# Top-32 attention and a tanh-shrink FFN: engine order written out by hand, search on pairs of keys, tanh subtraction on GpSimd

## The chip, the cores and the metric

The kernel runs on one core of a Trainium2 chip, in float32 throughout. The metric is the device time of one execution in microseconds. Engines are named as in the profile: PE (TensorE matmuls), PEld (its weight loads), DVE (VectorE), ACT (ScalarE), POOL (GpSimd), SP (SyncE, here a queue for DMA issues).

## What is computed

```python
# q, k, v: (8, 8, 576, 64) float32: batches, heads, positions, head dimension
scores = (1/8) * q @ k^T
kth = 32nd largest of each row of 576 scores
scores = where(scores >= kth, scores, -1e9) - max of the row
attn = exp(scores) / (sum + 1e-9)
x = (attn @ v), transposed to (4608, 512)
# w_in (512, 2048), w_out (2048, 512): 64-bit floats
h = x @ w_in
out = (h - tanh(h)) @ w_out
```

## The kernel before, in words

The attention part is a row of 144 steps. A step is one block of 128 queries of two heads (a pair, `hp`) of one batch: 16 such steps in a batch, four query blocks for each of four pairs. 576 is 4 x 128 + 64, so the last 64 queries of two pairs are put together in a step of their own (`g.rem`), two of them in a batch.

`turn_kq` transposes keys and queries of a pair on PE. `scores` (L181) computes a step's scores for both heads into `scps`, a PSUM tile of four banks with one buffer (`sc_ps`), and ACT copies it to `sc` in SBUF. `top` (L200) finds the 32 largest of each row's 576 on DVE: four rounds of MAX8, which gives the eight largest, with a MATCH_REPLACE8 between rounds that overwrites those eight. For two heads that is 8 MAX8 and 6 MATCH_REPLACE8 on 576 elements. The 32nd is the threshold (`tb`, POOL); ACT and POOL push all scores under it far down (`z`), and ACT takes the exponential with its sum.

`weigh` (L240) transposes `z` on PE in nine blocks, through `zt`, PSUM tiles of one bank with two buffers (`zt_ps`, which `turn_kq` and `values` share); ACT copies them out (`et`, `e4`). After every second query block `values` (L276) multiplies with v (`av`), transposes the reciprocal sums (`rb`), and DVE writes the product into `xT`.

Two query blocks of all pairs make a unit of 256 columns for the FFN (384 where the remaining queries of two batches are added). `ffn_h` (L324) does four matmuls into an `hps` bank (two buffers, `h_ps`), ACT takes the tanh, and DVE subtracts it straight from PSUM:

```python
        nc.scalar.activation(th[:, 0:N], ps[:, 0:N], AF.Tanh)
        u.g[f] = gpool.tile([P, 3 * P], FP32, tag="g", name="g")
        nc.vector.tensor_tensor(u.g[f][:, 0:N], ps[:, 0:N], th[:, 0:N], ALU.subtract)
```

`ffn_o` (L343) multiplies with `w_out` in `ops` tiles of the same two PSUM buffers. The weights come as 64-bit floats, and `load_weights` (L101) turns each of 32 pieces of 128 x 512 into float32 with four instructions on DVE, two on ACT and two on POOL; it runs beside the first steps, with its DMAs on ACT's queue.

A loop over n writes these functions down in the order scores(n+1), top(n), weigh(n-1), values(n-1), loads, and then FFN work up to a `credit` that grows by a share in each step. That is the order in which the framework is told of the instructions. It then orders each engine's queue itself, by its own planning, and sets the semaphores; in the trace, transposes of one step stand between FFN matmuls and scores of another.

Of the kernel before, what the change touches and what calls it, by code (L numbers as in the profile page):

```python
# [16 lines left out]
TOP = 32  # L17
# [13 lines left out]
class Unit:  # L31
# [3 lines left out]
    def __init__(self, name, blocks):  # L35
        self.name, self.blocks = name, blocks
        self.N = 128 * len(blocks)
        self.xT = None
        self.g = {}
# [3 lines left out]
def kernel(  # L43
# [16 lines left out]
    S2 = S // 2  # L60
    CD = DM // P
# [5 lines left out]
    assert D == 64 and R == 64 and DM == H * D and B % 2 == 0  # L67
# [19 lines left out]
    gpool = pool("g", 16)  # L87
# [5 lines left out]
    make_identity(nc, ident[:])  # L93
    w_in = [consts.tile([P, CD, DFF // WJ], FP32, name=f"w_in{j}") for j in range(WJ)]
# [6 lines left out]
    def load_weights(j, i):  # L101
# [6 lines left out]
        raw64 = rawpool.tile([P, NW, 2], U32, tag="raw64", name="raw64")  # L108
        nc.scalar.dma_start(raw64[:].rearrange("p n w -> p (n w)"), src.bitcast(U32))
        lo, hi = raw64[:, :, 0], raw64[:, :, 1]  # L110

# [16 lines left out]
        nc.gpsimd.tensor_tensor(dst, dst, f[:], ALU.mult)  # L128

# [28 lines left out]
    def turn_kq(b, hp):  # L158
        for name, dst in (("k", kT), ("q", qT)):
# [12 lines left out]
            for rows, o in [(half(0), 0), (half(1), R)] if name == "k" else [(slice(0, P), 0)]:  # L172
                nc.scalar.copy(d[rows, o : o + JP], ps[rows, :])
                o = 0 if o else JP
                nc.scalar.copy(d[rows, o : o + R], p4[rows, 0:R])

# [4 lines left out]
    def scores(n, g):  # L181
# [16 lines left out]
        st[n] = dict(sc=sc)  # L198

    def top(n):  # L200

        sc = st[n]["sc"]
        scf = sc[:].rearrange("p t s k -> p t (s k)")
        m = mpool.tile([P, 2, TOP], FP32, tag="m", name="m")
        cur = [scf[:, t, :] for t in range(2)]
# [12 lines left out]
        tb = mpool.tile([P, 2], FP32, tag="tb", name="tb")  # L218
        nc.gpsimd.tensor_scalar(tb[:], m[:, :, TOP - 1], BIG, None, ALU.mult)  # L219

        z = zpool.tile([P, 2 * S], FP32, tag="z", name="z")
        zv = z[:].rearrange("p (t k) -> p t k", t=2)
        den = mpool.tile([P, 2], FP32, tag="den", name="den")
        for t in range(2):
            nc.scalar.activation(zv[:, t, :], scf[:, t, :], AF.Relu, bias=tb[:, t : t + 1], scale=-BIG)  # L225
        nc.gpsimd.tensor_tensor(zv, scf, zv, ALU.subtract)  # L226
        for t in range(2):
            nc.scalar.activation(  # L228
                zv[:, t, :],
                zv[:, t, :],  # L230
                AF.Exp,
                bias=nb[:, t : t + 1],
# [3 lines left out]
        st[n].update(z=z, den=den)  # L236
# [3 lines left out]
    def weigh(n, g):  # L240


        z, den = st[n]["z"], st[n]["den"]
        if g.rem:
            et = etrpool.tile([P, 2, J, P], FP32, tag="etr", name="etr")
            e4 = etrpool.tile([P, P], FP32, tag="e4r", name="e4r")
            o = 0
        else:
            o = (g.qt % 2) * P
            if o == 0:  # L250
                ets[g.hp] = (
                    etpool.tile([P, 2, J, 2 * P], FP32, tag="et", name="et"),
                    etpool.tile([P, 2 * P], FP32, tag="e4", name="e4"),
                    xpool.tile([P, 2, 2], FP32, tag="rd", name="rd"),
                )
            et, e4, rd = ets[g.hp]
            rd = rd[:, g.qt % 2, :]
        for t in range(2):
# [6 lines left out]
            nc.scalar.copy(et[:, t, :, o : o + P], zt[:].rearrange("p (c j) -> p c j", c=J))  # L265
        zt = zt_ps.tile([P, 512], FP32, tag="zt", name="zt")
        nc.tensor.transpose(zt[:, 0:P], z[:, JP : JP + P], ident[:])
        nc.scalar.copy(e4[:, o : o + P], zt[:, 0:P])
        if g.rem:
            rd = xpool.tile([P, 1, 2], FP32, tag="rdr", name="rdr")  # L270
            nc.gpsimd.tensor_scalar(rd[:, 0, :], den[:], EPS, None, ALU.add)
            return et, e4, rd
        nc.gpsimd.tensor_scalar(rd, den[:], EPS, None, ALU.add)
        return ets.pop(g.hp) if o else None

    def values(g, et, e4, rd):  # L276

        ri = xpool.tile(list(rd.shape), FP32, tag="ri", name="ri")
        nc.vector.reciprocal(ri[:], rd[:])
        rx = xpool.tile([P, 2, 2, D], FP32, tag="rx", name="rx")  # L280
        nq = 1 if g.rem else 2
# [183 lines left out]
```

## Time and profile before

| | |
|---|---|
| time, median of three runs | 2197.74 us (2193.26 to 2206.97) |
| profiled execution, its own time | 2196.81 us |
| its span in the trace | 2195.0 us |
| mean granted clock of TensorE in the span | 0.907 |
| busy share of the span | PE 82%, DVE 74%, ACT 45%, POOL 29% |

The span is what the trace covers; the rest of the execution's time, 1.8 us, lies around it. The granted clock is 1 where the throttle lets TensorE run at 2.4 GHz and 0.5 where it lets it run at 1.2 GHz, so that 0.907 is a mean over stretches of either. A matmul's record is longer than its turn on the engine, since matmuls overlap: busy time counts a moment once, and the mean of one is longer than busy time by count.

### The profile page before, as it was taken

To read this page: it belongs to the slowest core of one execution; us is meant where nothing else is said; L and a number is where in the kernel's file an instruction comes from. 1 tells how busy PE (TensorE), PEld (TensorE's weight loads), DVE (VectorE), ACT (ScalarE), POOL (GpSimd) and SP (SyncE) were. 2 spreads that over 40 slices of the span, in tenths; PEclk is the share of its full clock that TensorE was granted. 3 is DMA by queue.
4 is the path that set the end of the run, shared out by engine and by line. 5 is a ranking of instruction groups with operands and counts; after the bars stand their busy time and mean duration, and the time that the engine had idled before them with its cause. 6 is when DMAs were issued, how large, how long until landed. Compare 5 with 4: busy or idle time off the path is not lost. (4 is left out here: it accounts for less than half of the span.)

```text
span 2195.0 us, 24121 instructions
## 1 busy us (share of the span) xinstructions
PE 1799.9 (82%) x8160; PEld 1035.6 (47%) x8160; DVE 1624.4 (74%) x3440; ACT 997.5 (45%) x2069; POOL 628.4 (29%) x726
## 2 busy tenths in 40 slices
PE   3354777988888888989888988989888988888879
PEld 2222534545454464545444464646444464646444
DVE  6777677887778786878778786878778776878730
ACT  4333444454454444544554454544445444544420
POOL 5555542222223222222222222222223222222210
PEclk7555897999889999999889999999979999999989
DMA  5211111000110001000110000100100000000000
GB/s 148 61 58 58 39 51 31 14 10 5 38 33 1 15 22 37 17 10 1 43 33 1 15 23 27 28 10 1 41 24 12 10 19 24 27 11 1 10 0 15
DMA packets 102140, 56.10 MB, mean 26 GB/s; under 512 B 85121, under 2 KB 93313, under 8 KB 102017
## 3 DMA queue, kind: packets, MB, share of 16 engines
q1 hardware_dynamic: 97408, 37.78, 6.6%
q10 hardware_dynamic: 4608, 16.78, 2.4%
q8 instruction: 65, 1.06, 0.2%
q14 instruction: 59, 0.48, 0.1%
HBM read 45.09 MB, written 9.44 MB: 25 GB/s over the span
## 5 line engine op out<-in xcount | busy, mean ns | idle before, releaser
L210 DVE MAX8 m<-w 128x8 f32<-128x576 f32 x864 | 616.0, 747 | 0.0
L347 PE MATMUL ops<-w_out,g 128*128 128x512 f32 x1152 | 537.4, 609 | 19.2 <-DVE g L339 9.6
L226 POOL TENSOR_TENSOR z<-sc,z 128x1152 f32<-128x1152 f32 x144 | 381.1, 2647 | 205.8 <-issue 153.8
L329 PE MATMUL hps<-xT,w_in 128*128 128x256 f32 x1536 | 392.7, 401 | 54.9 <-DVE g L339 40.5
L214 DVE MATCH_REPLACE8 w<-m,w 128x576 f32<-128x576 f32 x576 | 427.5, 742 | 0.0
L225 ACT ACTIVATE z<-sc,tb 128x576 f32<-128x576 f32 x288 | 208.7, 768 | 328.9 <-POOL tb L219 328.7
L228 ACT ACTIVATE z<-z,nb 128x576 f32<-128x576 f32 x288 | 220.9, 768 | 286.9 <-POOL z L226 286.9
L329 PEld LDWEIGHTS hps<-xT,w_in 128*128 128x128 f32 x1536 | 291.7, 201 | 115.2 <-DVE g L339 57.6
L347 PEld LDWEIGHTS ops<-w_out,g 128*128 128x128 f32 x1152 | 214.9, 197 | 233.0 <-issue 206.3
L210 DVE MAX8 m<-sc 128x8 f32<-128x576 f32 x288 | 207.1, 747 | 151.2 <-ACT sc L197 151.1
L262 PE MATMUL zt<-ident,z 128*128 128x128 f32 x1152 | 178.3, 299 | 147.5 <-ACT z L228 143.0
L219 POOL TENSOR_SCALAR tb<-m 128x2 f32<-128x2 f32 x144 | 47.4, 329 | 846.6 <-DVE m L210 761.0
L189 PE MATMUL scps<-kT,qT 64*128 64x288 f32 (+1 forms) x1280 | 247.4, 458 | 3.7 <-ACT sc L197 3.7
L262 PEld LDWEIGHTS zt<-ident,z 128*128 128x128 f32 x1152 | 137.3, 151 | 214.1 <-ACT z L228 165.6
L214 DVE MATCH_REPLACE8 w<-m,sc 128x576 f32<-128x576 f32 x288 | 211.7, 742 | 0.0
L197 ACT COPY sc<-scps 128x1152 f32<-128x1152 f32 x144 | 159.8, 1110 | 86.0 <-PE scps L189 81.5
L339 DVE TENSOR_TENSOR g<-hps,th 128x256 f32<-128x256 f32 (+1 forms) x256 | 113.8, 451 | 108.4 <-ACT th L337 106.7
L329 PE MATMUL hps<-xTb,w_in 128*128 128x384 f32 x512 | 186.5, 507 | 7.9 <-DVE g L339 7.2
L337 ACT ACTIVATE th<-hps 128x256 f32<-128x256 f32 (+1 forms) x256 | 100.5, 407 | 200.4 <-PE hps L329 196.7
L189 PEld LDWEIGHTS scps<-kT,qT 64*128 64x128 f32 (+1 forms) x1280 | 117.2, 186 | 114.8 <-issue 87.9
L291 PE MATMUL av<-et,vb 128*64 128x256 f32 x1024 | 143.9, 430 | 9.4 <-ACT et L265 9.3
L265 ACT COPY et<-zt 128x512 f32<-128x512 f32 x256 | 139.8, 586 | 4.9 <-PE zt L262 4.5
(60 smaller groups left out, 1196.6 us busy)
## 6 DMA issues: line engine op xcount, KB each, us to landing
raw<-in_moe_w_in_dram ACTq DMA_DIRECT2D x16, 512.0 KB, 4.4
kin<-in_k_dram SPq DMA_DIRECT2D x64, 128.0 KB, 2.6
qin<-in_q_dram SPq DMA_DIRECT2D x64, 128.0 KB, 2.6
vb<-in_v_dram SPq DMA_DIRECT2D x64, 128.0 KB, 2.2
raw<-in_moe_w_out_dram ACTq DMA_DIRECT2D x16, 512.0 KB, 3.2
out_dram<-ot SPq DMA_DIRECT2D x32, 256.0 KB, 2.3
kin<-in_k_dram SPq DMA_DIRECT2D x64, 16.0 KB, 2.3
qin<-in_q_dram SPq DMA_DIRECT2D x64, 16.0 KB, 2.4
```

The costliest lines, as they stand in the source:

```text
L189: nc.tensor.matmul(ps[rows, t, s, 0:S2], qT[g.b, g.hp + i][half(t), qs], kT[g.b, g.hp + i][half(t), ks], start=True, stop=True,)
L197: nc.scalar.copy(sc[:], ps[:, :, :, 0:S2])
L210: nc.vector.max(m[:, t, m8], cur[t])
L214: nc.vector.match_replace(w[:], m[:, t, m8], cur[t], NEG)
L225: nc.scalar.activation(zv[:, t, :], scf[:, t, :], AF.Relu, bias=tb[:, t : t + 1], scale=-BIG)
L226: nc.gpsimd.tensor_tensor(zv, scf, zv, ALU.subtract)
L228: nc.scalar.activation(zv[:, t, :], zv[:, t, :], AF.Exp, bias=nb[:, t : t + 1], scale=scale, accum_out=den[:, t : t + 1],)
L262: nc.tensor.transpose(zt[:, c * P : (c + 1) * P], z[:, m0 + c * P : m0 + (c + 1) * P], ident[:])
L265: nc.scalar.copy(et[:, t, :, o : o + P], zt[:].rearrange("p (c j) -> p c j", c=J))
L291: nc.tensor.matmul(av[half(t), cols], vb[g.b, hp][:, t, c, :] if c < J else vr[g.b, hp][rows, :], et[:, t, c, cols] if c < J else e4[rows, ...
L329: nc.tensor.matmul(ps[:, 0:N], w_in[j][:, c, fo : fo + P], u.xT[:, c, 0:N], start=(c == 0), stop=(c == CD - 1),)
L347: nc.tensor.matmul(acc[u, i][:], u.g[f][:, i * P : (i + 1) * P], w_out[part][:, f % FJ, :], start=(f == 0), stop=(f == CF - 1),)
```

## The change

**Order.** The loop body stands in `manual_schedule`, which keeps each engine's queue in the order written. In step n the order is: transposes of step n-2 (two of three groups), mask of n-1, search of n, half of the step's FFN items, scores of n+1, the third group of transposes of n-2, exponentials of n-1, a quarter of the items, values of n-2, loads and turns, the last quarter. The reciprocal of step n-2 (`invert`) stands in DVE's queue inside the search of n, after its first round. An FFN item is one `ffn_h` (four matmuls) or two f of an `ffn_o`; 4.4 are dealt in a step while there are any.

**Search.** The 576 scores of a row are taken as 288 pairs (column x with column x+288). DVE takes minimum and maximum of each pair, one operand from PSUM (`ps`) and one from SBUF, so `scps` is now held until DVE has read it. The four rounds run on the 288 larger ones, and the eight largest of the smaller ones are put in for the last round: 2 TENSOR_TENSOR, 10 MAX8 and 6 MATCH_REPLACE8. Should a row have more of the smaller ones among its 32 than the eight, that is seen at the end: `b8s` against `tbs`, summed by a matmul, loaded into registers as a flag; if it is set, the whole program runs a second time with the old search (`run(True)`).

**Subtraction on GpSimd.** ACT takes tanh of two f at once (512 columns), copies `hps` to SBUF as well, and POOL subtracts. POOL also writes `xT`, from a copy that ACT makes of `av` and the reciprocals together. The remaining queries get units of their own (four batches, 256 columns), so all 18 units have 256 columns.

**Weights.** `convert` is cut in three: the DMA (now on SP's queue), a first part up to POOL's limiting of the exponent, a second part. Three pieces end in a step, from step -1 to step 10; of three pieces in a row two have both parts in the same step.

```diff
-    rawpool = pool("raw", 2)
     ldpool = pool("ld", 1)
     kqpool = pool("kq", 4)
-    scpool = pool("sc", 2)
-    wpool = pool("w", 3)
-    mpool = pool("m", 4)
+    scpool = pool("sc", 3)
+    abpool = pool("ab", 2)
+    mpool = pool("m", 3)
     zpool = pool("z", 2)
-    etpool = pool("et", 2)
-    etrpool = pool("etr", 1)
+    etpool = pool("et", 1)
     xpool = pool("x", 2)
-    xbpool = pool("xb", 1)
+    xrpool = pool("xr", 1)
     hpool = pool("h", 2)
-    gpool = pool("g", 16)
+    thpool = pool("th", 3)
+    gpool = pool("g", 6)
...
+    def convert(j, i):
...
-        nc.scalar.dma_start(raw64[:].rearrange("p n w -> p (n w)"), src.bitcast(U32))
+        raw64 = gpool.tile([P, NW, 2], U32, tag="g", name="raw64")
+        nc.sync.dma_start(raw64[:].rearrange("p n w -> p (n w)"), src.bitcast(U32))
+        yield
...
-        f = rawpool.tile([P, NW], FP32, tag="f", name="f")
-        fu = f[:].bitcast(U32)
-        nc.vector.tensor_scalar(fu, hi, 20, 0x7FF, ALU.logical_shift_right, ALU.bitwise_and)
-        nc.scalar.activation(f[:], fu, AF.Copy, bias=-896.0 * 2.0**23, scale=2.0**23)
...
+    def search(n, exact):
+        x = st[n]
+        sc, ps = x["sc"], x.pop("ps")
+        m = x["m"] = mpool.tile([P, 2, TOP], FP32, tag="m", name="m")
+        ab = abpool.tile([P, 2, S + 8], FP32, tag="ab", name="ab")
+        if exact:
+            cur = [sc[:, t].rearrange("p s k -> p (s k)") for t in range(2)]
+            nxt = [ab[:, t, 0:S] for t in range(2)]
+            last = nxt
+        else:
+            x["ab"] = ab
+            cur = nxt = [ab[:, t, 0:S2] for t in range(2)]
+            last = [ab[:, t, 0 : S2 + 8] for t in range(2)]
+            hi, lo = ab[:, :, 0:S2], ab[:, :, S2 + 8 :]
+            nc.vector.tensor_tensor(lo, ps[:, :, 0, 0:S2], sc[:, :, 1, :], ALU.min)
+            nc.vector.tensor_tensor(hi, ps[:, :, 0, 0:S2], sc[:, :, 1, :], ALU.max)
+            for t in range(2):
+                nc.vector.max(ab[:, t, S2 : S2 + 8], lo[:, t, :])
         rounds = TOP // 8
         for i in range(rounds):
             m8 = slice(8 * i, 8 * i + 8)
             for t in range(2):
-                nc.vector.max(m[:, t, m8], cur[t])
+                nc.vector.max(m[:, t, m8], last[t] if i == rounds - 1 else cur[t])
             if i < rounds - 1:
                 for t in range(2):
-                    w = wpool.tile([P, S], FP32, tag="w", name="w")
-                    nc.vector.match_replace(w[:], m[:, t, m8], cur[t], NEG)
-                    cur[t] = w[:]
+                    nc.vector.match_replace(nxt[t], m[:, t, m8], cur[t], NEG)
+                cur = nxt
+            if i == 0:
+                yield
...
+                    tbs[:, t, n : n + 1],
+                    m[:, t, TOP - 1 : TOP],
+                    m[:, t, TOP - 9 : TOP - 8],
+                    BIG,
+                    ALU.min,
+                    ALU.mult,
...
+            nc.gpsimd.tensor_tensor(zv[:, t, :], scf[:, t, :], zv[:, t, :], ALU.subtract)
+        if not exact:
+            nc.gpsimd.tensor_scalar(
+                b8s[:, :, n], x.pop("ab")[:, :, S2 + 7], BIG, None, ALU.mult
+            )
+        x.update(z=z, zv=zv, nb=nb)
...
+    def invert(n):
+        g, rd = steps[n], rds.get(n)
+        if rd is not None and (g.rem or g.qt % 2):
+            nc.vector.reciprocal(rd[:], rd[:])
...
-        nc.scalar.copy(rs[:, 0:N], rb[:, 0:N])
+                av[:, 1, i * P : (i + 1) * P], rx[:, i].rearrange("p t d -> p (t d)"), ident[:]
+            )
+        xs = xpool.tile([P, 2, N], FP32, tag="xs", name="xs")
+        nc.scalar.copy(xs[:, :, 0:w], av[:, :, 0:w])
         if g.rem:
-            u = units[g.b | 1, 1]
+            u = rests[g.b // 4]
             for i in range(2):
-                o = 2 * P + (g.b % 2) * R
-                nc.vector.tensor_tensor(
-                    xt(u)[:, g.hp + i, o : o + R], av[:, half(i)], rs[:, half(i)], ALU.mult
+                o = g.b % 4 * R
+                nc.gpsimd.tensor_tensor(
+                    xt(u)[:, g.hp + i, o : o + R], xs[:, 0, half(i)], xs[:, 1, half(i)], ALU.mult
                 )
         else:
             u = units[g.b, g.qt // 2]
-            nc.vector.tensor_tensor(xt(u)[:, g.hp, 0:N], av[:, 0:N], rs[:, 0:N], ALU.mult)
+            nc.gpsimd.tensor_tensor(xt(u)[:, g.hp, :], xs[:, 0], xs[:, 1], ALU.mult)
...
-        th = hpool.tile([P, 3 * P], FP32, tag="th", name="th")
-        nc.scalar.activation(th[:, 0:N], ps[:, 0:N], AF.Tanh)
-        u.g[f] = gpool.tile([P, 3 * P], FP32, tag="g", name="g")
-        nc.vector.tensor_tensor(u.g[f][:, 0:N], ps[:, 0:N], th[:, 0:N], ALU.subtract)
-    acc = {}
+        if f % 2:
+            th = thpool.tile([P, 2, N], FP32, tag="th", name="th")
+            if f % FJ == 1:
+                u.g.append(gpool.tile([P, FJ, N], FP32, tag="g", name="g"))
+            g = u.g[-1][:, f % FJ - 1 : f % FJ + 1, :]
+            nc.scalar.activation(th[:], ps[:], AF.Tanh)
+            nc.scalar.copy(g, ps[:])
+            nc.gpsimd.tensor_tensor(g, g, th[:], ALU.subtract)
...
+        share = 1.1 * items * 2 * CF / NS
...
+        at(-6, lambda: load_kq(*pairs[0]))
+        for i, (b, hp) in enumerate(pairs):
             n = first[b] + 2 * hp
-            at(n - 6, lambda b=b, hp=hp: load_kq(b, hp))
-            at(n - 4, lambda b=b, hp=hp: turn_kq(b, hp))
+            turn = turn_kq(b, hp)
+            at(n - 4, lambda turn=turn: next(turn))
+            at(n - 3, lambda turn=turn: next(turn))
+            if i + 1 < len(pairs):
+                at(n - 3, lambda i=i: load_kq(*pairs[i + 1]))
             at(n - 2, lambda b=b, hp=hp: load_v(b, hp))
...
+        pieces = [] if exact else [convert(j, i) for j in range(2 * WJ) for i in range(FJ)]
+        for i, piece in enumerate(pieces):
+            for s in range(3):
+                at((i + s) // 3 - 1, lambda piece=piece: next(piece))
+        credit = 0.0
+        def deal(part):
+            nonlocal credit
+            credit += part * share
+            while work and credit > 0:
+                work.pop(0)()
+                credit -= 1
+            credit = credit if work else min(credit, 0.0)
+        for n in range(-6, NS + 2):
+            here = lambda i: 0 <= n + i < NS
+            if here(-2):
+                w = weigh(n - 2)
+                next(w)
+            if here(-1):
+                mask(n - 1, exact)
+            if here(0):
+                s = search(n, exact)
+                next(s)
+                if here(-2):
+                    invert(n - 2)
+                next(s, None)
+            elif here(-2):
+                invert(n - 2)
+            deal(0.5)
+            if here(1):
+                scores(n + 1)
+            if here(-2):
+                next(w)
+            if here(-1):
+                expo(n - 1)
+            deal(0.25)
+            if here(-2):
+                values(n - 2)
+            for fn in todo.pop(n, []):
+                fn()
+            deal(0.25)
+        while work:
+            work.pop(0)()
+        return NS
+    with tc.manual_schedule():
...
+        NS = run(False)
+    bad = xpool.tile([P, 2, NS], FP32, tag="bad", name="bad")
+    nc.vector.tensor_tensor(bad[:], b8s[:], tbs[:], ALU.is_gt)
+    any_bad = xpool.tile([P, 1], FP32, tag="anybad", name="anybad")
+    nc.vector.reduce_max(any_bad[:], bad[:].rearrange("p t n -> p (t n)"), axis=mybir.AxisListType.X)
+    cnt = zt_ps.tile([P, 512], FP32, tag="zt", name="cnt")
+    nc.tensor.matmul(cnt[0:1, 0:1], any_bad[:], ones[:], start=True, stop=True)
+    flag = xpool.tile([1, 1], I32, tag="flag", name="flag")
+    nc.vector.tensor_copy(flag[:], cnt[0:1, 0:1])
+    again = nc.values_load(flag[0:1, 0:1], min_val=0, max_val=P)
+    with tc.If(again > 0):
+        with tc.manual_schedule():
+            run(True)
```

## Rows read from the trace of the kernel before

**Rows 1.** Page of before: busy us (share of the span) xinstructions.
```profile
PE 1799.9 (82%) x8160; PEld 1035.6 (47%) x8160; DVE 1624.4 (74%) x3440; ACT 997.5 (45%) x2069; POOL 628.4 (29%) x726
```

**Rows 2.** Windows, search instructions of L210 alone: start:end, us, busy (count), clock.
```profile
0.00:300.00 300.00, 75.78 (x106) 0.70 0.23 70
600.00:2000.00 1400.00, 571.38 (x804) 0.95 0.07 19
```

**Rows 3.** Windows of all engines: start:end, us, busy (count) by engine, clock.
```profile
600.00:2000.00 1400.00, 1222.67 (x5701) 707.65 (x5697) 1088.16 (x2320) 672.08 (x1404) 350.76 (x457) 0.95 0.07 19
602.00:634.00 32.00, 27.26 (x116) 16.30 (x115) 23.56 (x53) 16.42 (x34) 7.45 (x10) 0.73 0.15 38
2124.80:2190.00 65.20, 65.20 (x173) 32.40 (x171) 5.57 (x10) 6.07 (x12) 0.00 (x0) 1.00 0.02 8
```

**Rows 4.** Waits of PE from 600 to 2000 us: total us, times, longest.
```profile
PE zt L267 <- ACT et L265: 50.0, 29, 5.2
PE zt L262 <- ACT z L228: 28.7, 14, 5.0
PE hps L329 <- DVE g L339: 26.7, 26, 2.1
```

**Rows 5.** Groups by form, 600-2000 us: count, busy us, mean ns, idle.
```profile
L210 DVE MAX8 m<-w 128x8 f32<-128x576 f32 x604 | 431.9, 747 | 0.0
L347 PE MATMUL ops<-w_out,g 128*128 128x512 f32 x800 | 371.4, 605 | 7.3 <-DVE g L339 7.3
L214 DVE MATCH_REPLACE8 w<-m,w 128x576 f32<-128x576 f32 x403 | 299.2, 742 | 0.0
L329 PE MATMUL hps<-xT,w_in 128*128 128x256 f32 x1096 | 273.3, 395 | 23.3 <-DVE g L339 19.5 <-DVE xT L314 3.6
L226 POOL TENSOR_TENSOR z<-sc,z 128x1152 f32<-128x1152 f32 x101 | 265.6, 2630 | 138.7 <-issue 113.4 <-POOL nb L217 25.2
...
L329 PE MATMUL hps<-xTb,w_in 128*128 128x384 f32 x376 | 137.7, 504 | 7.2 <-DVE g L339 7.2
...
L265 ACT COPY et<-zt 128x512 f32<-128x512 f32 x178 | 97.1, 585 | 1.3 <-PE zt L262 1.0
...
L339 DVE TENSOR_TENSOR g<-hps,th 128x256 f32<-128x256 f32 x136 | 56.2, 419 | 37.9 <-ACT th L337 36.9
...
L339 DVE TENSOR_TENSOR g<-hps,th 128x384 f32<-128x384 f32 x48 | 26.0, 548 | 25.0 <-ACT th L337 24.8
```

**Rows 6.** Timeline 1000 to 1032 us: one run of FFN matmuls at full clock.
```profile
1009.66 5.45 PE L329 MATMUL hps<-xT,w_in 128*128 128x256 f32 x24 [1.52 <-DVE g L339]
```

**Rows 7.** Groups of the weight conversion, whole span.
```profile
L122 POOL TENSOR_SCALAR f<-f 128x512 int32<-128x512 f32 x32 | 62.1, 1950 | 15.1 <-ACT f L121 13.6
...
L125 DVE SCALAR_TENSOR_TENSOR f<-raw,f 128x512 uint32<-128x512 uint32 x32 | 30.9, 967 | 78.6 <-POOL f L122 78.4
...
L128 POOL TENSOR_TENSOR w_in<-w_in,f 128x512 f32<-128x512 f32 x16 | 20.7, 1292 | 5.3 <-DVE f L125 5.1
...
L121 ACT ACTIVATE f<-f 128x512 f32<-128x512 uint32 x32 | 19.1, 617 | 6.7 <-DVE f L120 6.6
...
L120 DVE TENSOR_SCALAR f<-raw 128x512 uint32<-128x512 uint32 x32 | 13.4, 419 | 0.0
...
L113 DVE SCALAR_TENSOR_TENSOR w_in<-raw,w_in 128x512 f32<-128x512 uint32 x16 | 10.9, 682 | 0.0
...
L112 DVE TENSOR_SCALAR w_in<-raw 128x512 uint32<-128x512 uint32 x16 | 7.9, 496 | 8.8 <-DMA raw<-in_moe_w_in_dram 8.8
```

**Rows 8.** Timeline of the first 60 us: a DMA issue, the first search.
```profile
15.92 0.57 SPq L146 DMA_DIRECT2D qin<-in_q_dram  x1
...
24.64 1.41 DVE L210 MAX8 m<-sc 128x8 f32<-128x576 f32 x2
```

**Rows 9.** Timeline of PE, 2105 us to the end.
```profile
2107.34 42.04 PE L329 MATMUL hps<-xTb,w_in 128*128 128x384 f32 x120 [0.61 <-DVE xTb L309]
2149.21 41.36 PE L347 MATMUL ops<-w_out,g 128*128 128x512 f32 x96
```

More of the change, by code (lines that the diff above doesn't have):

```diff
@@ L60 @@
     S2 = S // 2
+    N = 2 * P
     CD = DM // P
@@ L175, in turn_kq, with scores @@
                 nc.scalar.copy(d[rows, o : o + R], p4[rows, 0:R])
+            yield
     st = {}
-    def scores(n, g):
+    def scores(n):
+        g = steps[n]
         ps = sc_ps.tile([P, 2, 2, 512], FP32, tag="sc", name="scps")
@@ new lines, in search, with mask @@
+            if i == 0:
+                yield
+    tbs = consts.tile([P, 2, B * NHP * J + 2 * B], FP32, name="tbs")
+    b8s = consts.tile([P, 2, B * NHP * J + 2 * B], FP32, name="b8s")
+    def mask(n, exact):
+        x = st[n]
+        sc, m = x["sc"], x.pop("m")
+        scf = sc[:].rearrange("p t s k -> p t (s k)")
+        if exact:
+            nc.gpsimd.tensor_scalar(tbs[:, :, n], m[:, :, TOP - 1], BIG, None, ALU.mult)
+        else:
+            for t in range(2):
+                nc.gpsimd.tensor_scalar(
[6 more added lines that the diff above has]
+                )
@@ L268, in weigh, with values @@
         nc.scalar.copy(e4[:, o : o + P], zt[:, 0:P])
[L269 to L279, printed above, removed]
+        st.pop(n)
+        yield
+    def values(n):
+        g = steps[n]
+        if not g.rem and g.qt % 2 == 0:
+            return
+        et, e4 = ets.pop(n)
+        ets.pop(n - 1, None)
+        rd = rds.pop(n)
+        nq = 1 if g.rem else 2
         rx = xpool.tile([P, 2, 2, D], FP32, tag="rx", name="rx")
-        nq = 1 if g.rem else 2
-        nc.gpsimd.tensor_copy(rx[:, 0:nq], ri[:].unsqueeze(3).to_broadcast([P, nq, 2, D]))
-        N = P if g.rem else 2 * P
-        av = zt_ps.tile([P, 512], FP32, tag="zt", name="av")
+        nc.gpsimd.tensor_copy(rx[:, 0:nq], rd[:].unsqueeze(3).to_broadcast([P, nq, 2, D]))
+        w = nq * P
+        av = zt_ps.tile([P, 2, N], FP32, tag="zt", name="av")
         for i in range(2 if g.rem else 1):
@@ L362, in ffn @@
         for f in range(CF):
-            yield CD * u.N, lambda f=f: ffn_h(u, f)
-        for i in range(len(u.blocks)):
-            for part in range(WJ):
-                yield FJ * DM, lambda i=i, part=part: ffn_o(u, i, part)
-    def block(b, qt):
-        return [(slice(0, P), out[b * S + qt : b * S + qt + JP : J, :])]
-    def rem_block(b):
-        return [(half(i), out[(b + i) * S + JP : (b + i + 1) * S, :]) for i in range(2)]
-    units = {}
-    steps, first, done = [], [], {}
-    for b in range(B):
-        first.append(len(steps))
-        for a in range(2):
-            blocks = [block(b, 2 * a), block(b, 2 * a + 1)]
-            if a and b % 2:
-                blocks.append(rem_block(b - 1))
-            units[b, a] = Unit(f"{b}{a}", blocks)
-            for hp in range(NHP):
-                steps += [Step(b, hp, 2 * a), Step(b, hp, 2 * a + 1)]
-                if a and hp % 2:
-                    steps.append(Step(b, hp - 1, J))
-            done[len(steps) - 1] = units[b, a]
@@ L409 @@
-    work = []
-    credit = 0.0
-    for n in range(-6, NS + 2):
-        if 0 <= n + 1 < NS:
-            scores(n + 1, steps[n + 1])
-        if 0 <= n < NS:
-            top(n)
-        if 0 <= n - 1 < NS:
-            g = steps[n - 1]
-            ready = weigh(n - 1, g)
-            st.pop(n - 1)
-            if ready:
-                values(g, *ready)
-            if n - 1 in done:
-                work += list(ffn(done[n - 1]))
-        for fn in todo.pop(n, []):
-            fn()
-        if work:
-            credit += share
-        while work and credit > 0:
-            cost, fn = work.pop(0)
-            fn()
-            credit -= cost
-        credit = min(credit, 0.0) if not work else credit
@@ L433, with plan, block, rem_block @@
-    for _, fn in work:
-        fn()
+            yield lambda f=f: ffn_h(u, f)
+        for i in range(2):
+            for part in range(CF // 2):
+                yield lambda i=i, part=part: ffn_o(u, i, part)
+    units, rests, steps, first, done, work = {}, [], [], [], {}, []
+    def plan():
+        units.clear(), rests.clear(), steps.clear(), first.clear(), done.clear()
+        def block(b, qt):
+            return [(slice(0, P), out[b * S + qt : b * S + qt + JP : J, :])]
+        def rem_block(b):
+            return [(half(i), out[(b + i) * S + JP : (b + i + 1) * S, :]) for i in range(2)]
+        for b in range(B):
+            first.append(len(steps))
+            if b % 4 == 0:
+                rests.append(Unit([rem_block(b), rem_block(b + 2)], "xTr"))
+            for a in range(2):
+                units[b, a] = Unit([block(b, 2 * a), block(b, 2 * a + 1)], "xT")
+                for hp in range(NHP):
+                    steps.extend([Step(b, hp, 2 * a), Step(b, hp, 2 * a + 1)])
+                done[len(steps) - 1] = units[b, a]
+                if a == 0:
+                    steps.extend([Step(b, hp, J) for hp in range(0, NHP, 2)])
+                    if b % 4 == 3:
+                        done[len(steps) - 1] = rests[-1]
```

127 lines of the change are left out of this document (66 added, 61 removed).

## The prediction

> **What bounds the kernel now.** I read the page first [rows 1]: PE is busy in 82% of the span and DVE in 74%, so either may set the pace, and the rest is far below. A share over the whole span mixes stages, so next come the windows. The search tells where a step ends: eight MAX8 make a step. In the first 300 us there are 106 of them, 13.25 steps, some 20.8 us a step after the first search at 24.6 us [rows 2, 8]. From 600 to 2000 us there are 804, or 100.5 steps of 13.93 us [rows 2]. After the last step stands a tail of FFN matmuls alone, 42.0 and 41.4 us [rows 9]. So there are three stages with three limits.
>
> In the steady stage PE is busy 1222.7 of 1400 us, at a mean clock of 0.95 [rows 3]: 12.17 us a step, with 1.76 us idle. The waits say for what: the third group of transposes for ACT's copy of the first (50.0 us), the first group for the exponentials (28.7), FFN matmuls for the subtraction on DVE (26.7) [rows 4]. None is a shortage of an engine: they are waits in a queue, and the last is one behind the search, as DVE runs MAX8 without a gap [rows 5]. DVE has 1088 of 1400 us, 10.8 a step. So PE with its waits sets the steady stage, DVE and the weights set the start, PE alone the tail.
>
> **DVE, part by part.** A MAX8 on 576 elements takes a turn of 431.9/604 = 0.715 us, a MATCH_REPLACE8 0.742 [rows 5]. No row shows either on 288. The nearest rows with two lengths on this engine are the subtractions: 419 ns on 256 and 548 on 384, 1.01 ns an element [rows 5]. By that 288 elements fewer save 0.29 us, and the new turns are 0.425 and 0.45. The other bound is that length does not count, 0.715 and 0.742. I take the lower, since 576 elements in 0.715 us are themselves near 1 ns each. Minimum and maximum read 576 elements with one operand in PSUM, as the subtraction does: 548 + 192 x 1.01 = 742 ns each. The search becomes 10 x 0.425 + 6 x 0.45 + 2 x 0.742 = 8.4 us a step, 13.1 by the other bound. It was 8 x 0.715 + 6 x 0.742 = 10.2. The subtractions and the products for xT leave DVE, about 140 us in all. DVE falls to 8.5 of a step that PE fills for 12, and leaves the path of the steady stage.
>
> **ACT and POOL.** ACT gains 144 copies of 512 columns at 0.585 us [rows 5], 84 us, and wider copies for xT, 20 us: from 997 to some 1100 us, half the span. POOL gains 144 subtractions of 512 at 1.28 us (the weights' product has that form [rows 7]), 184 us, the products for xT, some 50, and small operations, some 70: from 628 to some 930. The mask's subtraction, 2.63 us [rows 5], is cut in halves. All this lies beside PE. Its cover is that PE needs 12 us a step where ACT needs 7.7 and POOL 6.5; if the order put one of them behind the other with PE last, up to 2.5 us of a pair of f (tanh, copy, subtraction) would show, but two hps banks leave PE the next pair, 3.6 us, meanwhile. I cost it at nothing on that cover.
> The Trainium skill's page GPSIMD Engine Reference (4.1, Engine selection) advises against two-input elementwise work on GpSimd, as about twice slower than VectorE. The rows agree on the ratio, 1.28 us against an estimated 0.68 for 512 columns, but not on the price: the slower engine has the room. By the rule alone the move would cost 144 x 0.6 = 86 us if it stood on the path; I count none of it.
>
> **PE in steps 11 to 145.** Its work hardly changes: the units of 384 columns become units of 256. An ffn_h item is 8 matmul records (each matmul is two), an ffn_o item 4. At the clock of the steady stage they take 8 x 273.3/1096 = 1.99 and 4 x 371.4/800 = 1.86 us [rows 5]; at full clock 8 x 5.45/24 = 1.82 [rows 6] and 4 x 41.36/96 = 1.72 [rows 9], with the clock from [rows 3]. The rest of a step is (1222.7 - 371.4 - 273.3 - 137.7)/100.5 = 4.38 us [rows 3, 5], some 4.0 at full clock (an estimate by the same ratio). Counting the deal through the loop: steps 9 and 10 get 6 of 576 items, steps 11 to 145 get 520, and 50 are left for the tail. That is 520 x 1.93 + 135 x 4.38 = 1593 us at the old clock and 520 x 1.77 + 135 x 4.0 = 1460 at the full one. The clock falls where PE pauses: 0.73 in a stretch with 27 of 32 us busy, 1.00 where it is busy throughout [rows 3]. With fewer pauses it should stay near full; I take 1500.
>
> Of these 135 steps 115 have 4.3 items on average, 10 have two, 9 none and one a single one, because a unit comes every nine steps and is used up in seven or eight. A step without items is set by DVE, 8.7 us with a little slack, against 4.4 of PE: 9 x 4.3 + 10 x 0.8 + 2.5 = 50 us.
> The waits of rows 4 go: the third group of transposes now comes after two items and the scores, the first one a whole step after its exponentials, and hps banks are freed by ACT. What is late next: on odd steps q's transposes need the bank that the xT copy frees, 0.6 us after the last av matmul. I take 0.5 us for each of 115 steps, 57 us; the bounds are none and the old 1.76 us, 238 us over 135 steps.
>
> The added waits: PE's scores(n+1) now wait for DVE's minimum and maximum of step n, with two transposes, an item and the values queued behind. DVE starts search n as the last is done, half a step ahead, so this costs nothing while DVE's step is shorter than PE's. DVE's reciprocal inside the search waits for POOL's sum, and the rest of the search is queued behind it; by the written order the sum's exponentials end a few us after the scores copy that starts the search, about when its first round is over (2 x 0.74 + 4 x 0.425 + 2 x 0.45 = 4.1 us). A microsecond late would vanish in DVE's slack; nothing is counted, and the case of many is a rival.
>
> **The start.** The loads of the weights move from ACT's queue to SP's, behind q, k and v: an issue takes 0.6 us there [rows 8], 20 stand ahead of the first piece, and some of them wait for transposes. I estimate it 15 us later than now, but the first search, behind it on DVE, still at about 26 us (24.6 now [rows 8]). Then steps 0 to 10 each carry three pieces. On DVE a piece costs 0.42 + 0.46 + 0.68 + 0.97 = 2.5 us [rows 7], 7.6 a step. Two of three wait within themselves: after DVE's first operation ACT 0.62 and POOL 1.95, of which DVE fills 1.1 itself: 1.5 each, 3.0 a step (the whole wait was 78.4/29 = 2.7 before [rows 7]). Half a microsecond for a piece whose DMA is issued in the same step. So 8.4 + 7.6 + 3.0 + 0.5 = 19.5 us, and 26 + 11 x 19.5 = 240 us to the end of step 10; bounds 215 and 270. Before, step 11 came at about 24.6 + 11 x 20.8 = 253, so the start gives little.
>
> **Tail and end.** 50 items at 1.77 us: 88 us. The copy and the store of the last block take 2195.0 - 2190.6 = 4.4 us as now [rows 9]; the flag (a matmul, a copy, register loads, a jump) has no row: between nothing, beside the store, and 12 us; I take 5 more. The second pass does not run: counting pairs in the inputs of the reference, no row has more than 6 smaller ones among its 32 where 8 are allowed.
>
> **Sum.** 240 + 1500 + 50 + 57 + 88 + 10 = 1945 us of span, 1.8 around it: **1947 us**. The profiled execution before took 2196.8, which is 0.9 us under the median of 2197.74, so no correction. A change under 1% is not told from none here, as the three runs spread by 0.6%.
>
> **Rivals.**
> *PE has more room than its busy share says.* By the records PE is 87% busy, yet matmuls of 0.61 us take turns of 0.43 [rows 5, 9]; isolated groups carry an end that a closed row hides. At full clock throughout, no stalls and a start of 235: 235 + 1460 + 50 + 88 + 10 = 1843, and with 3.9 for the rest of a step **1830 us**. Against it: the runs before had gaps after the same groups for reasons of data. Chance 0.09. The Trainium skill's Perfetto Trace Analysis (Identifying the Most-Contended Engine) says that matmul busy time is no measure of the distance to the roofline and sends the reader to weight loads, here 47% [rows 1]; the tail, where busy time and turns agree, bears that out only in part.
> *The waits only change their names.* PE keeps 1.76 us idle a step: 240 + 1500 (1593 at the old clock) + 50 + 238 + 98 = **2126 to 2219 us**. For it: a queue written by hand stalls wholly where the planner would slip something else in. Chance 0.08, half of it within 1%.
> *The short search costs what the long one did.* DVE 13.3 us a step bounds all: 26 + 11 x 24.2 + 135 x 13.3 + 98 = **2186 us**. Against it the slope of rows 5. Chance 0.03.
> *DVE holds the scores bank.* If POOL's sum for the reciprocal stands behind its subtractions (2 x 1.28 + 2.6 + 1.1 = 6.3 us), the search stops for that long in its middle, the next minimum is late, and PE with it: 14.7 us a step, 26 + 11 x 25.8 + 135 x 14.7 + 98 = **2393 us**. It decides from 5.5 us of wait a step, where DVE's step passes 13.9. For it: one POOL queue serves both; against: the exponentials come after the mask's subtractions anyway. Chance 0.06.
> *The second pass runs after all:* some 3800 us, chance 0.01.
>
> **Chances.** The forecast, from 1855 to 2060, has 0.72; a remnant of 0.01 stays out. Faster by over 1%: 0.72 + 0.09 + half of the second rival + 0.01 of the third = 0.86; within 1%: the other half and 0.02 = 0.06; slower: 0.08. The range goes from 1855, which cuts a third of the first rival, to 2100, for a start of 270, the old clock and no longer stalls; what it leaves out sums to 0.2.
>
> **What would show it.** MAX8 at 0.43 us and DVE under 65% busy; steady steps of 12.2 us on average, PE over 93% busy in them and clock above 0.97; no wait of PE for DVE; waits of DVE on ACT's scores copy instead. Steps without FFN at 8.7 us. Step 11 at 240 us. Wrong if MAX8 is above 0.55 us, if PE's idle time a step stays over 1 us, or if DVE's reciprocal waits for POOL by microseconds.

## The result, and the profile after

The changed kernel takes 1871.84 us (median of four runs, 1869.99 to 1873.38) against 2199.65 for the kernel before in the same runs: a ratio of 0.851, 95% interval 0.848 to 0.854. The forecast was 1947 us, range 1855 to 2100.

The page's busy line answers to [rows 1]:

```profile
PE 1645.2 (88%) x8418; PEld 1048.9 (56%) x8418; DVE 1200.5 (64%) x3667; ACT 1066.4 (57%) x2101; POOL 954.0 (51%) x1399
```

PE has 155 us less busy time for the same products, DVE 424 less, POOL 326 more. The span is 323.4 us shorter: 154.7 us of that are busy time of PE, 168.7 idle time. PE's mean granted clock rose from 0.907 to 0.937 in the profiled executions, and its records stand closer together; what each is worth no run separates. Four windows follow: steps 11 to 145, a stretch of them with two steps that have no FFN items, a long stretch at full clock, and the tail (columns as in [rows 3]).

```profile
240.00:1776.00 1536.00, 1479.04 (x7778) 948.76 (x7778) 1022.62 (x3281) 951.20 (x1889) 786.62 (x1243) 0.98 0.09 22
303.00:335.00 32.00, 25.71 (x124) 15.28 (x124) 23.68 (x77) 22.16 (x47) 14.62 (x27) 0.88 0.26 65
758.00:1343.00 585.00, 574.05 (x2996) 365.79 (x2995) 379.38 (x1223) 353.45 (x701) 294.90 (x463) 1.00 0.08 22
1776.00:1865.00 89.00, 88.62 (x288) 53.38 (x284) 0.14 (x1) 13.54 (x25) 13.41 (x11) 1.00 0.04 9
```

Steps 11 to 145 take 1536 us, 11.4 us each where it was 13.93. PE is busy in 1479 of them and idle in 57. Some 29 of these 57 lie in ten steps without FFN items, which come in pairs, in five stretches like 303 to 335; elsewhere PE is 98% busy. From the start of the search of step 11 to that of the last step pass 1499 us (244 to 1743), in the kernel before 1846 (237 to 2084). So the whole gain lies there: the start is 7 us longer than before, and what follows the start of the last search 18 us. The waits that remain from 240 to 1776 us answer to [rows 4]:

```profile
PE av L363 <- POOL rx L346: 29.4, 20, 2.1
PE zt L325 <- ACT kT L179: 14.3, 7, 2.8
PE kqps L174 <- ACT xs L367: 6.2, 26, 0.2
```

None of the three of [rows 4] is left; the largest, 29 us, is new: the transposed reciprocals wait for POOL's copy. PE's scores also wait 143.7 us for DVE's minimum and maximum, but only before 244 us, in the stage that DVE sets. The groups that answer to [rows 5] and [rows 7], with these scores:

```profile
L235 DVE MAX8 m<-ab 128x8 f32<-128x288 f32 (+1 forms) x1152 | 467.0, 447 | 0.0
...
L238 DVE MATCH_REPLACE8 ab<-m,ab 128x288 f32<-128x288 f32 x864 | 376.2, 443 | 0.0
L197 PE MATMUL scps<-kT,qT 64*128 64x288 f32 (+1 forms) x1280 | 197.9, 464 | 143.7 <-DVE ab L228 143.7
...
L411 POOL TENSOR_TENSOR g<-g,th 128x512 f32<-128x512 f32 x144 | 183.3, 1273 | 182.5 <-ACT g L410 180.3 <-issue 2.2
...
L227 DVE TENSOR_TENSOR ab<-scps,sc 128x576 f32<-128x576 f32 x144 | 109.0, 757 | 490.0 <-ACT sc L205 437.9 <-POOL b8s L273 28.0 <-ACT e L332 13.5
...
L124 POOL TENSOR_SCALAR f<-f 128x512 int32<-128x512 f32 x32 | 67.2, 2101 | 25.1 <-ACT f L117 24.4
...
L129 DVE SCALAR_TENSOR_TENSOR f<-raw,f 128x512 uint32<-128x512 uint32 x32 | 22.8, 712 | 36.5 <-POOL f L124 36.5
...
L119 DVE TENSOR_SCALAR w_in<-raw 128x512 uint32<-128x512 uint32 x16 | 16.4, 1023 | 0.0
```

A short MAX8 takes a turn of 467.0/1152 = 0.405 us, so its time does follow its length. DVE's first operation of a search waits 438 us in all for ACT's copy of the scores: DVE has room. The conversion's masking of the high word, L119 (L112 before), went from 0.50 to 1.02 us for the pieces of `w_in`.

### The profile page after: what moved, and what is told of

Same layout as the page of the kernel before. It is cut to its first block, busy times and chain, and to the rows that moved or that the text cites. A ratio compares the mean times of both kernels' runs of the same rounds, so it can differ in the third digit from the quotient of the medians.

```text
span 1871.6 us, 25682 instructions
## 1 busy us (share of the span) xinstructions
PE 1645.2 (88%) x8418; PEld 1048.9 (56%) x8418; DVE 1200.5 (64%) x3667; ACT 1066.4 (57%) x2101; POOL 954.0 (51%) x1399
## 4 chain that ended last, share of the span: by engine, by line
PE 79%; POOL 7%; ACT 6%; DVE 5%; issue 2%; SPq 1%; DMA 1%; ACTq 0%; POOLq 0%
PE ops L417 26%; PE hps L397 25%; PE scps L197 9%; PE av L355 8%; PE zt L325 7%; POOL f L124 2%; POOL z L271 2%; ACT z L284 2%; PE av L363 2%; PE zt L331 2%; ACT xs L367 1%; DVE f L129 1%; DVE m L235 1%; ACT sc L205 1%; DVE ab L238 1%
## 5 line engine op out<-in xcount | busy, mean ns | idle before, releaser
L271 POOL TENSOR_TENSOR z<-sc,z 128x576 f32<-128x576 f32 x288 | 399.3, 1408 | 235.2 <-ACT z L268 235.2
L235 DVE MAX8 m<-ab 128x8 f32<-128x288 f32 (+1 forms) x1152 | 467.0, 447 | 0.0
L227 DVE TENSOR_TENSOR ab<-scps,sc 128x576 f32<-128x576 f32 x144 | 109.0, 757 | 490.0 <-ACT sc L205 437.9
L397 PEld LDWEIGHTS hps<-xT,w_in 128*128 128x128 f32 x2048 | 384.0, 193 | 51.6 <-POOL xT L377 3.1
L238 DVE MATCH_REPLACE8 ab<-m,ab 128x288 f32<-128x288 f32 x864 | 376.2, 443 | 0.0
L197 PE MATMUL scps<-kT,qT 64*128 64x288 f32 (+1 forms) x1280 | 197.9, 464 | 143.7 <-DVE ab L228 143.7
L411 POOL TENSOR_TENSOR g<-g,th 128x512 f32<-128x512 f32 x144 | 183.3, 1273 | 182.5 <-ACT g L410 180.3
L268 ACT ACTIVATE z<-sc,tbs 128x576 f32<-128x576 f32 x288 | 208.4, 776 | 34.3 <-POOL tbs L255 34.3
L355 PE MATMUL av<-et,vb 128*64 128x256 f32 (+1 forms) x1536 | 153.5, 344 | 0.0
L409 ACT ACTIVATE th<-hps 128x512 f32<-128x512 f32 x144 | 85.6, 594 | 111.9 <-PE hps L397 107.7
L355 PEld LDWEIGHTS av<-et,vb 128*64 128x64 f32 x1536 | 88.1, 141 | 68.9 <-ACT e L332 23.1
```

Of the source, the lines that this page charges most:

```text
L197: nc.tensor.matmul(ps[rows, t, s, 0:S2], qT[g.b, g.hp + i][half(t), qs], kT[g.b, g.hp + i][half(t), ks], start=True, stop=True,)
L235: nc.vector.max(m[:, t, m8], last[t] if i == rounds - 1 else cur[t])
L238: nc.vector.match_replace(nxt[t], m[:, t, m8], cur[t], NEG)
L271: nc.gpsimd.tensor_tensor(zv[:, t, :], scf[:, t, :], zv[:, t, :], ALU.subtract)
L355: nc.tensor.matmul(av[half(t), 0, cols], vb[g.b, hp][:, t, c, :] if c < J else vr[g.b, hp][rows, :], et[:, t, c, cols] if c < J else e4[ro ...
L397: nc.tensor.matmul(ps[:, f % 2, :], w_in[j][:, c, fo : fo + P], u.xT[:, c, :], start=(c == 0), stop=(c == CD - 1),)
```

## Experiments

Theory A is the prediction's: PE sets the pace, and the written order keeps it fed. Each run below was timed beside the kernel before, whose median stayed between 2199.6 and 2203.6 us. The intervals of the ratios reach some 0.3% to either side, so that two runs less than some 10 us apart are not told apart.

**The long search back** (e1).

```diff
+    nc.gpsimd.memset(b8s[:], NEG)
...
-                mask(n - 1, exact)
+                mask(n - 1, True)
             if here(0):
-                s = search(n, exact)
+                s = search(n, True)
```

> The changed kernel with the long search (8 MAX8 and 6 MATCH_REPLACE8 on 576) put back, order and subtraction as changed; the scores bank is freed by ACT's copy again. Theory A (PE sets the pace and the written order keeps it fed; the short search only takes DVE off the path in the start and in steps without FFN): DVE 10.3 us a step stays under PE's 11.7, so 20 us more in the start, 16 us in nine steps without FFN, some tens where short steps of 9 us follow one another: 1910 to 1950 us. Rival B (the gain is the shorter search): 2100 us or more.

1886.5 us, ratio 0.856 (0.853 to 0.859): 15 us more, less than theory A's least. From 600 to 1600 us PE's busy time is the same as with the short search, though DVE's goes from 668 to 851 us:

```profile
600.00:1600.00 1000.00, 963.68 (x5043) 611.06 (x5040) 850.90 (x1793) 614.47 (x1221) 450.00 (x627) 0.99 0.09 24
```

Rival B falls. The loss is in the start: the search of step 11 begins at 262 us, in the changed kernel at 244, and from there to the last search a step takes 11.34 us, in the changed kernel 11.35.

**The subtraction back on DVE** (e2).

```diff
-            nc.scalar.copy(g, ps[:])
-            nc.gpsimd.tensor_tensor(g, g, th[:], ALU.subtract)
+            nc.vector.tensor_tensor(g, ps[:], th[:], ALU.subtract)
```

> The changed kernel with the tanh subtraction back on DVE, straight from PSUM, without ACT's copy. Theory A: in the written order the subtractions of a step stand behind a whole search on DVE, so the hps banks come free late and the next search waits for PE's last item; about 0.5 to 1 us a step of PE idle time: 1930 to 2000 us, with PE's longest waits on the subtraction. Rival B: DVE has room (8.4 us and 1.4 more in a step of 11.7), so no change: 1865 to 1885 us.

1874.9 us, ratio 0.851 (0.849 to 0.854): no difference, where theory A wanted 60 to 130 us. Rival B's range held. PE's waits for the subtraction are 3.0 us from 300 to 1700 us:

```profile
PE hps L397 <- DVE g L410: 3.0, 10, 0.3
```

**The framework's order** (e3).

```diff
-    with tc.manual_schedule():
-        NS = run(False)
+    NS = run(False)
...
-        with tc.manual_schedule():
-            run(True)
+        run(True)
```

> The changed kernel with manual_schedule taken away, so that the framework orders the queues itself; the instructions are the same. Theory A: PE's waits in its queue come back, 1.2 to 1.8 us a step: 2030 to 2120 us. Rival B (lighter DVE is what counts, whatever the order): 1900 us or less.

1849.1 us, ratio 0.840 (0.837 to 0.842): 23 us *faster* than the written order. Theory A in its main point is refuted: the framework orders the same instructions at least as well. Little of the difference lies in the start: the first operation of step 11's search (L227) stands at 240 us against 244, that of the last step at 1718 against 1743. So a step takes 11.20 us against 11.35, which makes 20 of the 25 us between the two profiled executions. The two rows of this run and of the changed kernel:

```profile
239.75 0.74 DVE L227 TENSOR_TENSOR ab<-scps,sc 128x576 f32<-128x576 f32 x1
...
1717.94 0.76 DVE L227 TENSOR_TENSOR ab<-scps,sc 128x576 f32<-128x576 f32 x1 [4.28 <-ACT sc L205]
```
```profile
244.22 0.74 DVE L227 TENSOR_TENSOR ab<-scps,sc 128x576 f32<-128x576 f32 x1
...
1742.85 0.76 DVE L227 TENSOR_TENSOR ab<-scps,sc 128x576 f32<-128x576 f32 x1 [4.39 <-ACT sc L205]
```

**The short search alone, in the kernel before** (e4). The edit puts `search` of the change into `top`, without the flag: a row with more than eight smaller ones among its 32 is not seen to.

> The kernel before with the search on pairs alone, ordered by the framework; rows with more than eight smaller ones among their 32 are not seen to (the inputs have none). Theory A: DVE falls to 9 us a step, the waits for the subtraction shrink, those for the exponentials and transposes stay: 2100 to 2180 us. Rival B: most of the gain of 328 us is here: 1930 to 1980 us.

2144.8 us, ratio 0.974 (0.971 to 0.977), 58 us of 328. Theory A's range held. From 600 to 1600 us DVE falls to 625 us busy and PE stays at 871; the wait is of 300 to 1700 us:

```profile
600.00:1600.00 1000.00, 871.09 (x4097) 505.95 (x4097) 625.03 (x1952) 488.17 (x1012) 283.10 (x403) 0.95 0.07 20
```
```profile
PE zt L283 <- ACT et L281: 122.4, 73, 2.8
```

So a lighter DVE alone leaves PE waiting, now above all for ACT's copies of the transposes. Neither search, nor subtraction, nor who writes the order down brings the gain by itself. What is left is the loop itself, whose order also guides the framework: **theory C**, the number of steps between a result and its use, or the place of the FFN items. Rival D: the form of the items.

**The loop of before with the changed instructions** (e5), **items in a lump** (e6), **depth one** (e7), all ordered by the framework. The bodies, in short:

```diff
 e5: scores(n + 1); search(n); mask(n); expo(n); weigh(n - 1); invert(n - 1); values(n - 1); loads; deal(1.0)
 e6: as changed, but
-            deal(0.5) / deal(0.25) / deal(0.25)
+            deal(1.0), once, at the end of the step
 e7: as changed, but
-    weigh(n - 2), mask(n - 1), expo(n - 1), invert(n - 2), values(n - 2)
+    weigh(n - 1), mask(n), expo(n), invert(n - 1), values(n - 1)
```

> The changed kernel's instructions, buffers and items, told to the framework in the order of the loop before (scores n+1, search, mask and exponentials of n, all transposes and values of n-1, loads, then the step's FFN items in one lump), ordered by the framework. Theory C, after the first four runs (what counts is how many steps lie between a result and its use and where the FFN items stand, since the framework takes the told order as its guide): PE's waits for the first copies and exponentials come back, 2050 to 2150 us. Rival D (what counts is what the items are: two f in a bank, evicted by ACT, units all of 256 columns; the framework finds an order for them): 1850 to 1880 us.

> Ordered by the framework, with the changed loop but all FFN items of a step in one lump at its end. Theory C, if the place of the items counts: 1930 to 2050 us, PE waiting for the first copies before its third group of transposes. If the depth alone counts, or rival D: 1845 to 1870 us.

> Ordered by the framework, with the items dealt in three parts as changed, but mask and exponentials in the step of their search and transposes and values one step after, as before. Theory C, if the depth counts: 1900 to 2050 us, PE waiting for exponentials. If the place of the items alone counts, or rival D: 1845 to 1870 us.

e5 2102.0 us, ratio 0.955 (0.952 to 0.958); e6 1839.0, 0.836 (0.833 to 0.839); e7 2046.2, 0.930 (0.927 to 0.934). Theory C holds in its half on depth: with the search a step nearer to the mask, the same instructions lose 197 us (e7 against e3). e5 loses 263 us to e6, but scores and transposes also stand in another place in its body. Nor do the 56 us between e5 and e7 show what the place of the items is worth at depth one, since the same places differ there. At depth two a lump is 10 us better, where the two intervals still overlap. Windows of e5 and e6, and who waits in e5:

```profile
600.00:1600.00 1000.00, 880.72 (x4352) 543.97 (x4350) 570.40 (x1824) 542.03 (x1055) 441.46 (x688) 0.96 0.08 20
```
```profile
600.00:1600.00 1000.00, 976.50 (x5142) 633.52 (x5141) 674.11 (x2169) 635.74 (x1249) 513.97 (x815) 1.00 0.09 24
```
```profile
DVE rd L303 <- POOL rd L298: 197.3, 31, 10.2
...
PE zt L331 <- ACT et L328: 98.0, 55, 3.3
```

PE is busy 881 of 1000 us in e5 and 977 in e6. In e5 DVE, busy only 570, stands 197 us before a reciprocal whose sum is still on its way, with the search queued behind; PE stands 98 us before the third group of transposes. In e7 the same wait of DVE, and what PE waits for most, from 600 to 1600 us:

```profile
DVE rd L303 <- POOL rd L298: 164.1, 33, 5.9
```
```profile
PE av L355 <- ACT e L332: 54.2, 28, 3.8
```

In e3 DVE's wait is 0.5 us in the same stretch. Exponentials and sums are told one step ahead of their use at either depth. What depth two adds is a step between the search and the mask: from the start of a step's search to its first transposes pass 27 us in e3 and 16 in e7 (means of steps 50 to 129).

**The kernel before in its written order** (e8).

```diff
+    ctx.enter_context(tc.manual_schedule())
     for n in range(-6, NS + 2):
```

> The kernel before, its queues kept in the order in which its loop is written. ACT's copies of the transposes of n-1 then stand behind mask and exponentials of n, and FFN items behind those, so a step is a chain: search 10.2, mask 4.1, exponentials 1.6, copies 1.4, values 3, items 8 us. Theory C: 25 to 30 us a step, 3300 to 4200 us. If the written order were as good as the framework's: 2200 us.

3903.7 us, ratio 1.774 (1.766 to 1.781), 27 us a step as expected. The framework had been worth 1704 us there. PE's longest wait from 600 to 1600 us:

```profile
PE zt L267 <- ACT et L265: 402.7, 35, 15.8
```

**Depth two alone, in the kernel before** (e9).

```diff
-    scpool = pool("sc", 2)
+    scpool = pool("sc", 3)
...
-    etpool = pool("et", 2)
+    etpool = pool("et", 1)
...
-            g = steps[n - 1]
-            ready = weigh(n - 1, g)
-            st.pop(n - 1)
+            mask(n - 1)
+        if 0 <= n - 2 < NS:
+            g = steps[n - 2]
+            ready = weigh(n - 2, g)
+            st.pop(n - 2)
```

> The kernel before with the loop alone changed: mask and exponentials a step after their search, transposes and values two steps after it (one et buffer less, one sc buffer more for the space); long search, subtraction on DVE, units of 384, items in a lump, ordered by the framework. Theory C (the depth is what feeds PE): DVE needs 10.9 us and PE 12, so 1900 to 1990 us. Rival E (depth helps only with the lighter DVE and the new items): 2100 us or more.

2034.5 us, ratio 0.924 (0.921 to 0.927): 168 us of 328 by the loop and the buffers that it needs, between C and E. The buffers alone do not do it: e5 and e7 have the same number of `sc` and `et` at depth one, and stay slow. Busy windows:

```profile
600.00:1600.00 1000.00, 930.39 (x4392) 536.06 (x4390) 851.38 (x1820) 521.61 (x1084) 276.02 (x360) 0.97 0.08 20
```

**Both DVE parts back, in e6** (e12): the edits of e1 and e2 together.

> The run with items in a lump (depth two, ordered by the framework, 1839 us) with both the long search and the subtraction on DVE put back: DVE gets 10.3 + 1.3 us a step or more, against PE's 11.1. It is to say what is left between the kernel before with the depth alone (2034 us) and 1839 us. If DVE's load is it, harmless in each half but not in both: 1930 to 2030 us, DVE over 88% busy and short of gaps. If the form of the items is it (two f in a bank, av and reciprocals in a bank, units of 256): 1850 to 1890 us.

1898.7 us, ratio 0.863 (0.861 to 0.865): between the two cases.

```profile
600.00:1600.00 1000.00, 965.14 (x5043) 615.40 (x5040) 897.55 (x1870) 588.43 (x1140) 345.65 (x544) 1.00 0.09 24
```

DVE is busy in 898 of 1000 us and PE still in 965. So DVE's load costs 60 us at depth two (e12 against e6). Of the 55 us between the profiled executions 27 lie in the start (the search of step 11 begins at 267 us against 239) and 28 after it (11.35 us a step against 11.14). What is left between e9 and e12 is 136 us: in e12 a step takes 11.35 us against 12.71, while start and tail are longer. In e9 an hps record of 256 columns takes 0.254 us of PE at a clock of 0.97, in e12 0.232 at 1.00, and PE is idle 0.9 us a step against 0.4. The two differ in the form of the items (evictions of 512 columns, units of 256, one bank for av and reciprocals), but also in the places of scores, transposes and reciprocals in the loop, in POOL's product for xT and in the pieces of the weights. Which of these does it no run separates.

**The start, and the deal** (e10, e11), from e6.

```diff
 e10:
-        nc.gpsimd.tensor_scalar(
+        nc.vector.tensor_scalar(
             f[:].bitcast(I32), f[:], 0.0, 255.0 * 2.0**23, ALU.max, ALU.min
 e11, besides:
-        share = 1.1 * items * 2 * CF / NS
+        share = 1.0 * items * 2 * CF / NS
```

> The fastest version so far (items in a lump, ordered by the framework), with the limiting of the exponent in the weight conversion moved from POOL (2.1 us) to DVE. If the start is set by DVE's waits for that operation and by DVE operations stretched beside it, 3 to 4 us a step for 11 steps: 1790 to 1810 us, and the stretched operations on DVE back at 0.42 and 0.68 us. If DMA or POOL sets the start: 1835 to 1845 us.

> The same with 4.0 items dealt in a step in place of 4.4, so that hardly a step goes without FFN items. If PE's remaining idle time lies in those steps (some 25 us): 15 to 25 us less than the run without it. If the framework had filled them from other steps already: within 5 us of it.

e10 1824.8 us, ratio 0.829 (0.826 to 0.832): 14 us, where 29 to 49 were expected. Of the 17 us between the profiled executions 14 lie in the start (the search of step 11 begins at 225 us against 239). DVE no longer waits for POOL, but its operations stay stretched, L124 itself to 1.09 us where it takes 0.42 undisturbed:

```profile
L124 DVE TENSOR_SCALAR f<-f 128x512 int32<-128x512 f32 x32 | 34.7, 1085 | 15.1 <-ACT f L117 15.1
...
L119 DVE TENSOR_SCALAR w_in<-raw 128x512 uint32<-128x512 uint32 x16 | 11.5, 718 | 0.0
```

e11 1806.8 us, ratio 0.821 (0.818 to 0.823): 18 us less, as the first case had it. This is the fastest version of the study, 65 us under the changed kernel. A step takes 10.96 us against 11.12 in e10, and from 600 to 1600 us PE is busy 985.5 us; what follows the start of the last search is 5 us longer.

## Why the prediction was right, point by point

**The bound and the terms.** PE sets the steady stage, as forecast. The sum was 1945 us of span. Measured were 240 us for the start (240; the search of step 11 begins at 244), 1479 of PE's work in steps 11 to 145 (1500), 57 of its idle time there (50 + 57), 89 and 7 for tail and end (88 and 10): 1871.6. The largest miss is the idle time, 50 us, the next PE's work, 21. The tail shows that FFN turns are shorter than the forecast took them (as [rows 9]):

```profile
1809.24 27.79 PE L397 MATMUL hps<-xT,w_in 128*128 128x256 f32 x128
1836.87 27.63 PE L417 MATMUL ops<-w_out,g 128*128 128x512 f32 x64
```

128 records of 256 columns take 27.79 us, 0.217 each, where the forecast took 5.45/24 = 0.227 [rows 6] from a short run, in which the overhang of the last record counts. Over 260 items x 8 records this makes 21 us. That PE's work fell short by as much is chance: the 1500 was a choice between 1460 at full clock and 1593 at the old one, and with 0.217 the full clock gives 1439, 40 under the 1479 measured at a clock of 0.98. Both terms of idle time came at about half: 29 us in the ten steps without items (50 for the short steps), which take 7.7 to 10.1 us, 8.8 in the mean (8.7), and 28 in the other steps (57). Of these 28, 20 are the wait for POOL's copy; the one that the forecast named, q's transposes behind the xT copy, is 6.2 us in all.

**DVE.** The slope held: 0.405 us for a turn, forecast 0.425; the lower bound was the right one. DVE left the path (64% busy, against 65 forecast at most). But its part in the gain is 15 us (e1, written order), or 60 with the subtraction (e12 against e6, the framework's order).

**ACT and POOL.** The subtraction on POOL costs nothing that can be told, as forecast (e2); it takes 1273 ns for 512 columns. The reason given for a gain, hps banks freed by ACT, is refuted by the same run. But what is left of PE's idle time are waits for copies on POOL and ACT, which the forecast did not name but for one.

**The waits go.** They do, but the reasons given carry only in part. The one that carries is the further step in the loop: with mask and exponentials in the step of their search 197 us come back (e7 against e3). A whole step between exponentials and transposes, as the forecast put it, did not come of it in the written order: the exponentials end 2.9 us before the first transposes on average (10.7 in e3). The two items ahead of the third group are not needed under the framework's order (e6). That the order is written by hand, which the change puts first, costs 23 us here (e3), though it is a good order: the old loop as written takes 3904.

**The start** came out as forecast by luck. The steps with three pieces are 0 to 9, not 0 to 10: one piece ends in step -1 and one in step 10. These ten take 20.55 us each (19.5) and step 10 takes 9.1, so that the eleven make 214.5 us, the forecast's sum. In such a step the search takes 7.6 us (8.4), DVE's work on three pieces 9.8 (7.6), since L119 and L120 are stretched to 1.09 and 1.06 us on average (the last section), and the wait within the pieces (L129) 36.5/32 = 1.1 us a piece (1.0). The first search starts at 29.7 us, not 26.

**Rivals.** *More room than the busy share says* (1830 us) came nearer than the forecast itself, by 42 us against 75: PE's turns were shorter and its stalls half, though not nothing. The Trainium skill's Perfetto Trace Analysis (Identifying the Most-Contended Engine) would judge by weight loads, beside the share of the peak. In the tail, where PE is busy in 88.6 of 89 us, they are busy in 53.4, so by them PE would still seem to have room; the trace agrees only that busy time alone is no measure, as PE's fell by 155 us for the same products. The others did not occur; the reciprocal of *DVE holds the scores bank* does wait, but only at depth one (197 us of 1000 in e5, 164 in e7).

## What to carry to other kernels

When several engines wait for one another though none is full, move the use of a result one whole step further away in the loop before shortening instructions; here that alone gave half the gain. Everything else that is new gave 98 (e5) to 153 us (e7) without it. A framework that orders queues follows the order it is told, so the loop's depth matters even where it reorders; written order and planned order should both be run. Before moving work between engines, look at whether the engine it leaves has gaps: in the changed kernel the shorter search was worth 15 us and the moved subtraction nothing that can be told, both together 60 at depth two.

## What the hardware showed that was not expected

In the start a DVE operation beside POOL's two-input products is stretched far beyond its own time:

```profile
23.36 0.42 DVE L119 TENSOR_SCALAR w_in<-raw 128x512 uint32<-128x512 uint32 x1
...
27.18 1.31 POOL L132 TENSOR_TENSOR w_in<-w_in,f 128x512 f32<-128x512 f32 x1 [0.88 <-DVE f L129]
27.27 1.50 DVE L119 TENSOR_SCALAR w_in<-raw 128x512 uint32<-128x512 uint32 x1
```

L119 takes 0.42 us alone, and 1.50 when it starts just after POOL's product has begun, ending 0.28 us after it. The Trainium skill's GPSIMD Engine Reference (8, Key points) says that GpSimd shares its SBUF interfaces with VectorE, with contention for DVE instructions in a two-port mode or with two SBUF inputs. L119 has one input, so by that page it would run in such a mode, which no run here shows. With the limiting on DVE (e10) L119 still takes 0.72 us on average for `w_in`: the 9 of all 32 that begin while POOL runs an operation of two inputs take 1.50 to 1.63 us, the other 23 0.42. MAX8 takes 0.45 us on average in either case, so that of DVE's work the search is not touched.
